# A Conformer block on one core: every engine's instruction order and the PSUM banks re-drawn

## The chip, the core and the metric

The kernel runs on one core of one Trainium2 chip. The core has five instruction queues that run at the same time and meet only at semaphores: TensorE (PE, matrix products into PSUM), VectorE (DVE), ScalarE (ACT, here mostly exponentials and tanh), GpSimd (POOL) and SyncE (SP, which here issues transfers). The metric is device time in microseconds for one execution, the median of several runs; less is better.

## The reference

Two sequences of 4,000 tokens with 144 channels go through one Conformer block. All inputs are bf16.

```
x = x + 0.5 * silu(layernorm(x) @ w_ff1a) @ w_ff1b          # 144 -> 576 -> 144
q, k, v = split(layernorm(x) @ w_qkv)                        # 4 heads of 36
p = softmax(q k^T / sqrt(36))                                # 4000 x 4000 for each head
x = x + (p v) @ w_o
a, b = split(layernorm(x) @ w_pw1);  h = a * sigmoid(b)
c = depthwise_conv(h, dw, 5 taps)
x = x + silu(c) @ w_pw2
x = x + 0.5 * silu(layernorm(x) @ w_ff2a) @ w_ff2b
out = layernorm(x)
```

## The kernel before

**Tiles.** The 8,000 tokens are 16 chunks of 500, eight for each sequence; a chunk is four blocks of 125 tokens. Keys come in tiles of 64. A score tile is one chunk of queries against one key tile for all four heads. PE makes it with four matmuls of 64 x 64 weights and 500 columns ("quads", tiles PS<-QT,KT in the profile), two per PSUM bank, so a score tile fills a pair of banks. Most score tiles are emptied by one ACT instruction of 128 x 1000 exponentials (PT<-PS). About one tile in five goes to DVE instead, which makes the exponential from integer operations in five instructions. PE then multiplies PT by the values (PS<-PT,VA, also quads) into banks 6 and 7, where a chunk's attention is summed. Banks 0 to 5 serve all else.

**Between the score tiles** lies the rest of the block for other chunks: feed-forward (`ff`, `ff_tile`, lines 1208 to 1260; tiles XT, WA, HT, WB), projections (`pre2`), the gated convolution (`glu`, `conv`) and the output half (`post1`, `post2`). Normalization (`ln`, line 1109) takes its statistics on DVE (ST), its square root and scaling on POOL (RS, XN). The transposed copy of a chunk (XT, XTQ) is made by a transpose on DVE and a round trip of transfers that SP issues: XN or AN to a DRAM buffer called rows, and rows to XT (`blocks`, line 1032).

**Order.** The program is recorded, not issued directly. A scheduler in the kernel (`pick`, line 1940) chooses step by step what comes next, and `Rec.op` records each instruction with its engine, its step number and its dependencies. All instructions of one engine that were recorded in one step are a block. There are 2,855 blocks on PE, 1,093 on ACT, 1,689 on DVE, 125 on POOL and 157 on SP. Then `Rec.reorder` (line 281) moves the blocks within each engine by a written table, ORDER: one character per block, whose place in ALPHABET less 45 is the number of places that the block moves (P is no move, `~` opens a longer number).

```python
shift.append(c - 45)
...
at[i + shift[i]] = blk
```

The second table, PLACES, gives each of the 1,724 PSUM tiles its first bank, one digit per tile (`place`, line 257). `reorder` reads off PE's new order which tile had a bank before, and makes the new tile's matmuls wait for the instructions on other engines that use the earlier tile:

```python
prior[k] = {last[b] for b in self.tiles[k] if b in last}
...
for p in prior[k]:
    o.deps += [(d, False) for d in users[p]]
```

`finish` (line 365) turns dependencies into semaphore waits, and `replay` (line 409) issues each engine's list in order. [...] All instructions are issued from line 419, so the profile gives that line nearly everywhere and tiles tell the groups apart.

Of the kernel before, what the change touches and what calls it, by code (L numbers as in the profile page):

```python
# [13 lines left out]
H = 4  # L14
# [26 lines left out]
        "nXMJ@LJMFMYGaJNKMJhLLLLljKKKKKKWKMMWNKK`BJJJQRecHFSIGKH]QKMRGKPMJJMMQTNPNXTRSUJUJJJSLPMPPQUQQNKOTOOR"
        "OQLPPPPPYOOPN[NNNOMfRNLYULMIMOS^KIMOJNaNNQMNHPPaUOMQNYKPSPPQUSVV^QQ^_Q5<@QCPMKIMNNTQMSMNSNUOYQKMMOQQ"
        "^MSOORNOPPCOORPZP^O]OOO[OCNOQEHMUJNNTOMR[MQWXMPMMNNDMPXSNNZMMTMMMTMPLMPP]OOOOQQNUKNOMQMP]WNOMPNVKYPN"
        "JNQHNOOPQQQMPPQOPUP]MNNNOOTNNOMNWOPPMPNOW]VNN[MMHMKYMMQ]YKI`JLQYJJKV[KHMJTLJOJPMQORPVMQNYMN]MN[bLLLL"
        "LMNLPRPKWOYFMNOVNOHXXMKOLNNNN[[_MMMTLLTKKKLJOOPRP`MO_OMNOMPQLLMRMMMPPPQOSYP[MOOISOLNPPIPSPTOLRNNWPNO"
        "QQMMPUQRN[QQQRJFPPPPJQQSPPKQQNPPPPVPPQOPVXOOPNDNPRROSVSYNFWMPYUPNDPJFPNPTOPYOLOPNQ[NLNRPMRLNNOPhUNZM"
        "MMNLNNPMMWYLPNZKNLMF[LPPSLVINLNOMWQNYPYPLQHKOSNORPGPPPS[OOLOOPPYLNNNVOMNOM^QMNTOO_KMMNOMPPLPNQOYL]RY"
        "LMKLMMPLY]KLNNQXMRXSLI[MDObNOENPMMNSNNQMMWNNNOSVNiKZNNQOTFNNOMXXUMMMM?TLLIYMQXXLLMMQZMJJ`ORLMUMKQYNL"
        "INPMMUVNLNOMYPMOORNNRUNKPNO_ROQLSSKMQMKPROLPSOORNOSOOOTVNNNNSNTMTMNNOVXNOMORLSNVXIMSYLMKLN^XYNLMNHMM"
        "WLLMXMNYMOLNNXMNXMMVMM[SLJLLZN^OLNNJUbLLLQNLPRGNNOOOPNRNOPPPeOOOOPSOOORROf`OPNO^@QDLJLMOLTKLTMTRKGMQ"  # L50
        "QNUOPNROYYPZOHNbILLLLbTLLSLLLLPLM_M[MMMMMcMMMMNLMOdZMNNNNIMMMMXMNNVOMKMMZNOUaMMMQMM]^HOMKNNNJZMKM[LM"
        "QgLLLMWMMMMU]LLLV^MQJMWTMHBHMZSKL[PLLZTMK_bMMIGbMPLPQMSVCKRKSMBINPPSPVOLOOOOZQNNS[MMMMNSMOMNO]aNNcMM"
        "MMMMMMNLNNNZWNZMZPNKPMYBENOPJYNNPMPQOLQNPPRRO[YQJNOPQOPXFPHPNOOOPWOOOOOOXPMTQOLOK^OXNNOMPPPLPPHQQNgR"
        "cOLQOMPNOOOOdRM@LdOJOIPIOOOJOOOOJOOPNUPNOOQQYLQ]NLZ[LLLdWKIKLLLWULE]LLLLLOMWRcKLLLNZM[PMMRILNKZJ`[JK"
        "MOLLUbKeJLLYKOUKMMMMMY=KMNNZNL^NLNNNNNN_NNNOQQNPTHNN_NLOOO^QMNPKO^QQM_JFPLOPJMNPPLPhMPROOPQOWOWNNNNU"
        "U?NO[HMTOOOCNOOOQO[OQOUOOOPHVORPYMGNPPMOVNN[QOVKPNZPGLOY]OPLOPPPBHOOORPRROR`OPWQNZCLNNPQZKMQETOJOMNU"
        "OOOOOPPPP[OOPNQNQRLMVZLOTNKPLLOOPPVPNOVOMRMOSLOOPPPPPZOWOMNNN]NLMPRTLNZUNLQMNYWNRAOPTOSHRNDQOPTOOPNP"
        "UOUQ_LROQQIQFNOYPNUKQNKTNKOQRSTNQNRXFQOQVQULMVEMPPP[PPPQODZcMPMMQINPKMPNOOOPRMNPPPQOZOOOOOQOMOOPXOOZ"
        "NNNNNN`NPWMXNNOPNKOCNOXPNOQOMZQMUOKXMZP[^XIMMOOKPABPJOPPPXOOQOPPPRIOPSOVSMOTKQUKLPNQNPXQOMROMPMQWQMU"
        "OQNJMQQNPQQTQOKTNO[NQOPQOUOOVRMUZPNVSYMN`OQK6TNNZ;NLNVMMMMTMMVWMMdMNLMNOO]N[MMM]XLJKKRK^aJHNPPRKNX>N"  # L60
        "OJLOMNPPPSPPQTVOOQVPLPQOAPQOPQOQZVOLOMRUMKL[MPMOOQWMMNNYOLNORNNNOYVNNNOWLMMROORROH]QNQMNOXNOMPMUPKMY"
        "NTOLORSTJMWOPPFObTYLNQSMKG_MKMNN`RMKLOLR]MKPNgIMMMNOYNKNNNNNZTMQXILIXJLMQLYOSJMNPU_]JLOKRSMMHLMOMQOW"
        "OOQOMOUNPNUQRM`YYLOREKNKKV[LJNLOSQJN`KPXLObLMWNK]MIJQLLOUO^LDLTKQNLVLQ^MMQRMSFMUWMNNWMG^MTRMJYLRPNGO"
        "TYMN[aXVMWQHKLJMFRf[M5LMNSNNKNLZMNNQRPLJTOIOO`^YMMNLMMOMKMMNRSLROLPPTOVOOLVNNPMOO_ROOLRNNNQQMMRNNPQO"
        "VQNNTVNLMPMZUO_QOLLOSNNVNOQNNQSPSWNWNPNVNN[QMNRPNQVXMNPMXPPXKUNNNNVQM~N?ZRMMMPXRLM]LLSMNLNQOMO[NQORO"
        "TNPPY[K]SBNNKILMNNPNPP_TNNOMN]NNNNNPMM_NNNNOQNQOPKWOOPKQN`YOOROOPFOQNROEQQUYJVNNPJOOJ[OOPNPROLYTNKMN"
        "TMNNNP^[NOMNNQMMOLNN]PNOOR[OPKQN_ZLNESMOOKHOM[NPPLPNOOPPMQSTMNPQQQQRSQRRTCQVNGRNOMTTTMMNUPPQHNQSPMYV"
        "TQKLLSSOIJPSSPTMKORNOQOPPPPPPSORNSMRNRRRNQQRPFRPQQQQQQRPFQO"
    ),
    "act": (  # L70
        "PPPPPPPPPPPPPRTNNOOPPQOPPPPPPXPNOSNNNNPPPPQOPPSPNOQZQORKRSLLOQQJPPPPQQNQOPPPPPPPPPQQQMPPQOPPPPPPPPRO"
        "OPQOPQQNPPPPPPPPPPPPPPPPPPPPPPPPPPPPPPPPPPPPPPPPPPPPPPPPPPPPPPPPPPPPPQOPPPROSNOOPPPPPPPPPQOPPPPPPPPP"
        "QOPPPPPPPPPPPQOPPPPPPPPPPPPQOPPPPPPPPPPPRPNPQOPPPPPRPNPPPPPPPPPPPPPPPPPPPPPPPPPPPPPPPPPPPPPPPPPPQOQQ"
        "NPPPPPPPPPPPPPPPPPPPPPPPPPPPPPPPPPPPPPPPPPPPPPPPPPPPPPPPPPPPPPPPPPPPPQOPPPPPPPPPPPPPPQOPPQOPPPPPPPPP"
        "PQOPPPPPPPPPPPPPPPPPPPPPPPPPPPROOPQOPPPPPPPPPPPPPPPPPPPQOPPPPQOPPPPPPPPPPPPPPPPPROOQQQMPPPPPPPPPPPPP"
        "PPPPPQOPPQOPPPPPPPQOPPPPPPPPPPQOPPQOPPPPQQQQQKQQNPPPPPPQOPPPPPPPPPPPPPPPQOPPPQOPPPPPPPPPPPPPPPPPPPPQ"
        "OPPPPPPPTOOOOROOPPPPPPPPPPPPPPPQOPQOPPPPPPPPPPQOPPQOPPPPPPPQOPPPPPPPPPPQOPPPPQOQOPPPPPPPPQOPPPPPPPPP"
        "QOPRPNQOPPPPPPPQOPPPPPPPPPPPPPPPPPPPPPQRNOPPPQOPPPPPPPQQNPPPPPPPPQOPPPPPPPQOQOPPQOPPPPPPPPPPQOPPPPPP"
        "PPPQOQOPPPPPPPPPPPPPPPPPPPPPPPPPQOPQQNPPPPPPPPPPPPPPPPPPPPROOPPPPPPPPPPPQQNPPPPPPPPQOPPPPPPPPPPPPPPP"
        "PPPPPQOPPPPPPPRPNQOPPPPPPPQOPPPPPPPPPPPPQOPPPPPPPPPPPPPPPPPPPPPPPPPPPPPPQOPPPPPPPPPPPPPPQOPPPPPPPPPP"  # L80
        "PPPPPPPPPPPPPPPPPPPPPPPPPPPPPPPPPQOSPNRNOQOUQNPMOPPPRORNQNPPPPPPQOROQQMPPPPPPQOPPPWORNNNOO"
    ),
    "dve": (
        "PUO[VM~P6~P6~P)~P6ILIKKLDKMJQRJJJKIKQKKLJKMKOLJWOILJHLJNQNPHFGNNNJMMMMBMWOIKIMINLMNOODNDPSPLORCFVSWC"
        "JDJSIOMBREEMKNCMMMMFNNJMMMMMMNLOPSPROLPPRPNPQOQOQQQMQOQQNPQQNQOPPQOPPQOPPPQOROOPROQVQOYPNOPROSPXURVQ"
        "UU;JNIQQSSSOSQRSSZRSSSKRVQUJ=OO)PROQNPRPRSLPRPQJQOPPPUOPNPQ`VPVOVOMEULFNKNRMRPQQQQIQOPQOQOSOORNTNOPN"
        "QOPQOPPQOQOPPPRPNPROQRMQRPQRPTPPPRPVVPNPSOLQQQQQQ5PPVPPPPPQRHQQQLPPPPPPPPQOPPPPPPPPPROSNPNPPPQSQSLSO"
        "RJQQLQQQQQQQQHPPROSPPTRPNQGQOPQOUQOPLQNRPNPQORUNNOOQNSOOTRUOMTOOPFPQOPPPPPPQQRRRKMRPNPQOPPPPPPPPPPQR"
        "PRPQQQHQOPWOPSOSKTLVOSNUNQMDOPPROOSOPNSQO^PjOOOSNNNCMNTMPLMNTNNNNNOOOPROOROOPRPQQRPJPRSNNQNPQOQOPQOQ"
        "OYRNNNYNOMNSOLRMULQNNOTPPMOQOQOPQOPPPSOPNSOSNPQLPPPPPPPVOOOOOXNOOROQNKUOOOOQNQOPPTTPNLNPPPPPPPPPPQSP"  # L90
        "PLQOPPP]OOOOOOOOOOOOQOQOPQOQOROOPQOWOPNOOOORPNPSPNSSPRSJTJWMRSLLRLMPTRNNQQLQOPPPPPPPPPQQSMPNPRPSPPQJ"
        "PPPPPQQNPQOQQNQOROOPQOPPPRPNPPPQQNPPPPTOOOOPQOPRPNQOQQRSOKQNQOSOOQNQRNOPQOSQRMMPPPPPROQNQOPPPPPQOPPP"
        "PQRPQRRORPQFPPPPPPPPPWPNPNOOOUPNOPNQSNSNNSNORNUQMPMOPROOROVNOOOPQMPPPPPPXQNQMQUNQNSOUQQUCOJOOPPQQNQO"
        "PPUPNOOOPPQRPQQRJQTPLOOTOOOOPPPQVNOQTMQNSQTNTFNNQNQOPPQQNPQOPPPQOQORPSPLOTOOOORORNQSMSNTRPRJRPIROQNQ"
        "OPTQNNTNOOSNSNNOUOOOOOPPPPPPROOROOQOQUROQSUSTGOHKPPPPPQOPQOQOPPQOPPROOQOPPPPPPPPPQRPUPPSORTRPRSUURXS"
        "=KQAQRNQQEPPPPPPPQOQOSOSOhTPMPRMSEOOKOPPPPPPROGNOPPPQRNRNOPQQQMPPPPPQQNQQNQQQQQKQQQRVOXOHOOLOOQNRPNP"
        "PPPPPPPSOOWNSNNQMUQKSOOQJQUN^PhLNKOPPKOKNNNPPMOOOOOOOOQQQRRKNPRPRPSQOQTPTODNRNQNQQUPLPROTRPWMXSNPSQW"
        "RZQUFOSDO7KOPPPTOOSOTOPPIPPPQOPPPPPPTPQMQMPQOPQQNQQRRORRRUQRPUWTQNRSCTRPRRRRDQQRPSPRSQR[RTQNPREO~NKO"
        "RNaNOOOPQMNQYNOPNPTQFNJPRRNNPPPPQOPQOPQOPRSOROUSINNNPPPPPPPPPPPQOPQOQQRPWQQNPTPUPUKOO?OPQOROQQMPQOPQ"
        "QNPQQSPTQNPHPPROOQSNPQULPNOORROQRPJPPSOOORO]SOSNPRWQQXPTRERGRRTTUXRTRSBSSSSSSSSAT@S&NNPPPPPPPPPPQO"  # L100
    ),
# [2045 lines left out]
```

## Time and profile before

| | |
|---|---|
| median of 3 runs | 874.99 us (874.88 to 875.48) |
| span of the profiled execution | 873.9 us; its own time is not given apart, so the runs' median stands for it, 1.1 us above the span |
| instructions | 27,051 |
| busy: PE, ACT, DVE, POOL | 844.3, 845.4, 824.8, 292.8 us |
| weight loads on PE (PEld) | 385.8 us busy |
| granted TensorE clock, mean | 0.998 |
| transfers | 28.82 MB in 114,353 packets, mean 33 GB/s |
| XT<-rows, time from issue to landing | 2.0 us (median) |

A row of the profile names the line, the engine, the operation and the tiles (out<-in), then how often it ran, its busy time and mean duration, and the idle time of the engine just ahead of it with what ended that. The chain of waits is followed back from the last instruction to whatever released each step.

### The profile page before, as it was taken

How to read it: one execution, taken by the hardware profiler on the slowest of the kernel's cores; microseconds unless marked ns; L12 is line 12 of the kernel's file. 1: busy time of each engine (PE TensorE's matmuls, PEld its weight loads, DVE VectorE, ACT ScalarE, POOL GpSimd, SP SyncE). 2: the span in 40 equal slices, each digit the busy share in tenths (PEclk: the TensorE clock that was granted, in tenths of full speed). 3: DMA queues.
4: the chain of work that ended last, by engine and by line, in shares of the span. 5: the costliest groups of instructions: out<-in, count | busy, mean ns of one | idle time of the engine just before them, and what ended most of it. 6: DMA issues, size and time to landing. Idle time of an engine off the chain costs nothing.

```text
span 873.9 us, 27051 instructions
## 1 busy us (share of the span) xinstructions
PE 844.3 (97%) x11419; PEld 385.8 (44%) x11419; DVE 824.8 (94%) x1821; ACT 845.4 (97%) x1098; POOL 292.8 (34%) x573
## 2 busy tenths in 40 slices
...
GB/s 100 49 62 29 23 17 44 33 67 30 29 52 39 17 50 11 45 22 47 23 4 29 24 56 17 30 30 16 37 31 24 21 31 21 19 15 38 28 26 35
DMA packets 114353, 28.82 MB, mean 33 GB/s; under 512 B 101090, under 2 KB 114230, under 8 KB 114230
## 3 DMA queue, kind: packets, MB, share of 16 engines
...
## 4 chain that ended last, share of the span: by engine, by line
ACT 59%; PE 25%; DVE 11%; POOL 4%; issue 1%; POOLq 0%; DVEq 0%
ACT PT L419 54%; PE PS L419 25%; ACT TH L419 5%; DVE PT L419 4%; POOL XN L419 2%; POOL RS L419 2%; DVE ST L419 2%; DVE X L419 1%; DVE XN L419 1%; DVE HT L419 1%; DVE U L419 0%; DVE KT L419 0%; DVE RS L419 0%; DVE AN L419 0%; DVE XT L419 0%
## 5 line engine op out<-in xcount | busy, mean ns | idle before, releaser
L419 ACT ACTIVATE PT<-PS 128x1000 bf16<-128x1000 f32 (+1 forms) x818 | 752.0, 1051 | 3.7 <-PE PS L419 2.8
L419 PE MATMUL PS<-QT,KT 64*64 64x500 bf16 x3968 | 419.9, 384 | 12.4 <-ACT PT L419 7.4
L419 PE MATMUL PS<-PT,VA 64*37 64x500 bf16 x4728 | 406.4, 372 | 1.6 <-DVE QT L419 1.0
L419 DVE TENSOR_SCALAR PT<-PS 128x500 int16<-128x500 f32 x380 | 250.2, 668 | 6.9 <-PE PS L419 5.1
L419 PEld LDWEIGHTS PS<-QT,KT 64*64 64x64 bf16 x3968 | 124.8, 104 | 232.0 <-ACT PT L419 132.2
L419 POOL TENSOR_SCALAR RS<-ST 125x4 f32<-125x4 f32 x130 | 37.8, 291 | 475.6 <-DVE ST L419 469.0
L419 PEld LDWEIGHTS PS<-PT,VA 64*37 64x37 bf16 x4728 | 142.7, 96 | 93.4 <-issue 13.6
L419 DVE TENSOR_SCALAR PT<-PT 128x1000 uint16<-128x1000 uint16 x380 | 154.2, 419 | 2.3 <-PE PS L419 1.0
L419 POOL TENSOR_SCALAR XN<-X,RS 125x144 bf16<-125x144 bf16 x260 | 144.7, 586 | 9.7 <-DMA out_dram<-XN 1.5
L419 DVE TENSOR_TENSOR PT<-PT 128x1000 bf16<-128x1000 bf16 x190 | 127.5, 674 | 0.9
L419 ACT ACTIVATE TH<-PS 128x500 bf16<-128x500 f32 (+3 forms) x194 | 102.8, 551 | 4.7 <-PE PS L419 4.5
L419 POOL TENSOR_TENSOR RS<-RS,NHALF 125x4 f32<-125x4 f32 (+1 forms) x93 | 92.8, 1002 | 33.5 <-DVE RS L419 27.9
L419 DVE SCALAR_TENSOR_TENSOR HT<-TH,PS 128x500 bf16<-128x500 bf16 (+1 forms) x135 | 81.0, 613 | 10.1 <-ACT TH L419 9.7
L419 PE MATMUL PS<-XT,WA 80*128 80x500 bf16 (+5 forms) x288 | 74.5, 364 | 4.2 <-DVE XT L419 1.0
L419 DVE BATCH_NORM_STATS2 ST<-X 125x6 f32<-125x288 bf16 x160 | 65.5, 446 | 1.6 <-DMA X<-in_x_dram 1.4
L419 DVE SCALAR_TENSOR_TENSOR X<-PS,X 125x288 bf16<-125x288 f32 (+1 forms) x128 | 56.6, 449 | 5.6 <-PE PS L419 4.3
L419 PE MATMUL PS<-WB,HT 128*125 128x144 bf16 (+1 forms) x640 | 52.6, 230 | 0.8 <-ACT HT L419 0.5
L419 PEld LDWEIGHTS PS<-WB,HT 128*125 128x125 bf16 (+1 forms) x640 | 44.3, 136 | 14.2 <-issue 4.3
L419 PEld LDWEIGHTS PS<-XT,WA 128*128 128x128 bf16 (+1 forms) x288 | 21.1, 97 | 37.7 <-issue 10.1
L419 POOL COPY U<-U 128x2 bf16<-128x2 bf16 (+1 forms) x54 | 12.0, 263 | 56.2 <-DVE U L419 56.2
L419 DVE STREAM_TRANSPOSE XN<-XN 128x320 f32<-128x320 f32 x54 | 27.0, 500 | 2.8 <-POOL XN L419 2.6
L419 PE MATMUL PS<-U,DG 128*128 128x250 bf16 (+6 forms) x204 | 28.8, 263 | 0.1
...
## 6 DMA issues: line engine op xcount, KB each, us to landing
...
```

The source lines that it names most:

```text
L419: ins = getattr(eng, o.name)(*o.a, **o.k)
```

## The change

Only the two tables differ: ORDER for all five engines and PLACES. The scheduler, the instructions, their operands other than the PSUM bank, the transfers and their number stay. The new tables come from a re-timing in which landings of transfers and waits carry a margin. Of 1,724 PSUM tiles, 683 have another bank.

```diff
 ORDER = {
     "pe": (
-        "PPPPPPPPQOPPPPROQNPPQRPQLPPRPTPUPNIZOVOKVVL~OOKOK~OUHINSNLMMMOPNOJSOOL[I[KMYMKOGRNJHFKOOOE^NNN_dMKLM"
...
+        'PPPPPPPPQOPPPQQQMPPPPPPPPSOUOMOYWMOX~OQQLHxSIYH~OXG~O[IIKSJKILJHKNOMOOQQXDYCOHNGOHX?FHHKLPLFnKPLe_KPMJUVJG=LJMFFPVlEoICKKLLRL_LMKNLRMRLMK[_Q'
...
     "pool": (
-        "PPPPPPPROOPPPSOPNPQQQQQQJPPPPPP_PPPPPJOOPQ[NKTMMOMNOSNUMNSNRNTKVNVMPLMPMROQTMOOTVMNNNOQTMOOQWMOOOSNN"
-        "NVOOPNOQNPPPRPQM"
+        'PPPPSOOQQMPPPSOPNQOPPPQQNPPPPPP^OOOOOTNOMQaLOPPIOOPPMOUNNPMVLU[MMMMQLNOPSOUKNOOSSMNNPQRNOPPSPNQQMPQQQMPPPSOOOPPPQRPM'
+        ''
     ),
     "sp": (
...
+        'PPPPPPPPQOPPPPPPPPPPPQQNQRSMNOPPPPPQOPPQOQOPPPPPSOOOPPPPQOPPSOOSNOOPPPQOPPPPPPSORNNPPVOPNSNNVMOOOOOPSOWNNOOOOOPROXNPNOOOORNOPPPQOROOPPPPPPPX'
+        'PNOOOOPQMPPPPPPQO'
+        ''
     ),
 }
 PLACES = (
-    "3054320451505435202310543130213550204405323242301405230054110122532155431241204124012410314032034023"
...
+    '43240510405134250421350102245231040421520105150412304523405004503101012141412340240014300442130242024305302341314010402430240213430532040324'
...
 )
```

More of the change, by code (lines that the diff above doesn't have):

```diff
@@ L39 @@
     "pe": (
-        "PPPPPPPPQOPPPPROQNPPQRPQLPPRPTPUPNIZOVOKVVL~OOKOK~OUHINSNLMMMOPNOJSOOL[I[KMYMKOGRNJHFKOOOE^NNN_dMKLM"
[L41 to L68, printed above, removed]
+        'PPPPPPPPQOPPPQQQMPPPPPPPPSOUOMOYWMOX~OQQLHxSIYH~OXG~O[IIKSJKILJHKNOMOOQQXDYCOHNGOHX?FHHKLPLFnKPLe_KPMJUVJG=LJMFFPVlEoICKKLLRL_LMKNLRMRLMK[_Q'
@@ new lines @@
+        'JhBIII[XKPHJ_JFLUIZKPMGLQMMWDNPRMOMTTZXTLPIKISOMJQQQT_QNIRTOM[OPFOJOQOQOIQO^QOMPNhNPNLZOLLPLWUNLNNZNaQNPQQCROHTQNROSKP[RRRYUPX]SGV`Q$HBQFFQK'
+        'PLOOTQMMRNRNTNSPMMTO`NXNOOOO_NNND^MMM_aYMILLHbKSHLIXHL^RMQMMa[YEP]MINTKNE6JKffLLXTLPLLLHLNPKMN`TNKNLQQQQEPQQX]SQJRLSWX`NPZ:OPEP@GNPQRLRPHQOb'
+        'TXMMMMRLOMTPPMGNUNPQOLR[_NOKNRWOQJKMSGbMKQOM`dPMKSXLIMKRHLIKLOOOTNXNNN^NNPMM]XMMMMMMNLPVOUYNYGLLQXMOLQFMYNQMNOO_W[LLLZLY]JJJJKMSXXYZFQOZK@MF'
+        '^dTXJ=LcHQJLRLaYHRAILWPKILMRCMMPVPNOPSWPZJOSINLMPUMUOOOPIUOOOOaPPSOJOPPKOOOVQNLMOXTXNNOPHUNIQSQKYKOW]PMVaNNKOETOUCXNH]PMXNODGNNOSQK^KOOOOOOO'
@@ new lines @@
+        'OOOOOPWOQNNWWNQOZZJM[EOMINOMRPRMREOUQNQXQMRPHMOQRPRKOPPPQSQOLPbQOQjKMNNNPMOLNQMMaOOQIMMNOMOOLPNPVPL[UULNKKM]OKTRLLMMP[MQTRLJQMKPUMP_MQMMWWNR'
+        'MOMKNRPSCRNfRRNNQOYFNNOMUNLMMMNSWMMQXLTOULIMORVSPM[N]NCOOLQTRMNIRHOU`OQLNLRORLMPPLPRMQRMOYQNNP^QUKOLJNPMeNWMMMXMPLLLYRLLMK^McL]LJNLa[MJ[PHJH'
+        'OTOJPZmBPAFOUYOVNK[PNK^BLNQM?ZLM_MGRMU^MGROKL[NAPL[SPZLHOPKVbDLMRMXVPKMUCL_LSKVGKMXMcLLLQLLLUUMa[NNPQ[HFYKMALLNXJLLOPSMSNSSN]QMPEO[QMYM[J]UK'
+        'ILIXLJTYLEMTLVN[EZLJ[LLZLLNK[UKN~OUMJDLNPaLPNJW[LMM[LLMKSDSI]KHMOFN`MTPTKIPRIRNHDMOPXaNNNTFNNNURGMMMUWNOJNSMN`QVNRIaN`QIL_GNN[MNHZL`LPLYUMO['
@@ new lines @@
+        ':OSKUM=LO<QagSNIMNOSQWNKKWMMMMXVMSOL:`SLP^MCOOOOOPQOSPRIZS@PNTPNSNSF^RdMHRPM]QHNP]GQHRIU[II^IIPKQJ]_KOTKWNFNIgOLPQRSUR@WTQU]LHR[KLR9TMK]^PhK'
+        'UNjdaSTOSWjbQ<SAZR?#>ZQ<P;TNBPWRPUUOUO6Q7UP7PRTZ^LaaMKMcLNLORK=MPNRHcL^SNL;LLOMSNcKMKLNXMRMMNTKNPK`K_WLM_OLJdXKXKIE^LJNLFOQQbTKKMM;SNNN[OZKN'
+        'LMMMNNNNZZNNZTMKWOJQQHRRFQSDOV[QObLOPGOPIOPPJVPbLPKSPJQIYLZMNLMTYWMI_HLGNLQLNOPNPNWNPUMNNNNUXNNN`MWNKPMVNNPULNDMSQXVJOOXORNFROOQbEOOOQOULNOa'
+        'NPMQNRFLQMQRVMNOHPQTPKRcNLOOOPNOO[NQMPPKVRIOKVYQ[SFOILYOQ]]MCMOMNPRMN@MPQOQOPVO]RMTRK[SIRTGaLOVENN]NCSSLMTMKWMTCLNRMMPVPVOLRTVXP^ZIOMUZMAL@T'
@@ new lines @@
+        'LQKSQRERH^QMNRTNXMNWHLOLSNJhMXVNNKMT^MMQNTaQNQBPPJQR=RYQNPT`H`OZPKQHNP3MPHTRXRMGGPNVOMQTRMTQIR[IPPKPPMR[OQWJOIRPLTQJ]THUO[T_HXHNORHNSCEKWRRR'
+        'XISOJRFMRPLROTNVSMRUKRLTTQFSTRUSFUURESUZESGIWSOJVSLLSMZRRS@WQNYOENFQOWKQ[LOTOMOOPVPNTOOOeZOO:QOMK]MMMMRNLXLLMcPLWIMM^WMNNKOSYKDLJUP]XKGMKOYL'
+        'U[^LWHLMVMNC_ULJMPUX^^Z]LLFM5LEOMEMI[SNNNNROMN[^NOTNIP]MJNIYWMPVOLFNTR[OCPFUYRTdSS[WRRRZQAYQ?SQ=KS;^R9Y[QUM`PTGXJGQRZVGQCKZQMVRPYL[OMQOT]QN!'
+        'SQNTYO4DNbWSMOMF[NPMOEPNWKOLROOTPGOOPPRPUPcPP[QKQEQMWRNGJMPJMRP^PPUUNZSMKM[PXMOQYMOk9MMPNOTPN8NaPXMUZMGLOHPPHORF[RDTPUOJ_YLMFLRMNNOJOOVPSOSO'
@@ new lines @@
+        '[_PYUOC]ZMILNK]Od]OVZQ7QLN;PXZRWOZ[IXM7NIYZ`L[KKQdLLOKQU^L%RJN&JSaLLM[L[NGOLLMOMUMMQGSMSNNOPXOZNROLPKVKOM[WNNV[MGNSM]MWQOQDPPVPPb[P:RSNNSNVX'
+        'MM8OULUXNOXO9PNOZRO]eKNNTNTUZLJLMS`RMAcLVNORVZLCLNRRL~NH]RKBLSQXLUQUJHKKVLUUMMMNURVTRL_WQYRPU[>EWNHPRH<NHPZ[NNRMNPMJNNOXOQWNLOOL_OPKP_bNOTI`'
+        'PSXGQGRREJRCJTAXORNXcHSQJLRKHMPPWPSJPMURP]FOUQOMPNPUP>UPR_L^GLXO_NJMPL_RJLRHOTOQ^I_:OJQOYPKOFKPMOQQQQSSUNBWOQSTOTRSTTBSSGBRKRSOPQJTTQSSTJJJQ'
+        'NP[VNPNLNOPSKNNQRPXLOPNOOOOPRROMTQNPMSORNRRRNQQSQFSPPQQQQQQEPQO'
@@ L69 @@
+        ''
     ),
     "act": (
[L71 to L80, printed above, removed]
@@ L81 @@
-        "PPPPPPPPPPPPPPPPPPPPPPPPPPPPPPPPPQOSPNRNOQOUQNPMOPPPRORNQNPPPPPPQOROQQMPPPPPPQOPPPWORNNNOO"
+        'PPPPPPPPPPPPPPSOOOPPPPPPPSOVNWOLNTMMNNPQOQORSQUUKKUNTMUNHMOOQQQMPPPPPROOROQNPPPPPQQQQLPPPQOPPPPPPPQOPPQOQQQMPPPPPPPPPPPPPPPPPPPPPPPPPPPPPPPP'
+        'PPPPPPPPPPPPQQNPPPPPPPPPPQQQMPPROQNPROOPPPPPPPPPPPPPPPPPPPPPQOPPPPPPPPPPPQOPPPPPPPPPPPPPPQQQMPSOOOPQRPMPQOPPPPPRPNPPPPPPPPPPPPPQQNPPPPPQQNPP'
+        'PPPPPPPPPPPPPPPPQOPPPPQOPPPPPPPPPPPPPPPPPPPPPPPPPPPPPPPPPPPPPPPPPPPPPPPQQQMPROOPPQOPPPPPPQOPPPPPPPPPPPPPPROQQQLPPPPPPPQQQQLQRNQNPQQNPQOPPPPP'
@@ new lines @@
+        'PPPPQOPPPPQOPPPPPPPPPPPPPPPQOPPPPPPPPPPPPRPNPPPPPPPPPPPPPROQNQQQRRKQQQKPPPPPPPPPPPPPPQOPPQOPPPQQRMOPQQNPPQQRRSSJRRRISSPSSSSJSBSTIQLQQQQQHPPP'
+        'PPPPPPPPPPPPPPPPPROQQMRROQQQJPPPPPPPPQQQMPPPPPPPTOOOOROOPPPPPPPPPPQOPPQOPQOPPPPPPPPPPPQOPPQOPPPPPPQQNPQQQMPPPPPPPPQQQMPPPPPPPPPPQQNPPQOSOOOP'
+        'PPPSPNOPPPPQQQQQKQOPQQNPQQNPPPPPPPPPPPQTNOPNQQNPPPPPPPQQNPPPPPPPQQNPPPPQOQOPPPPPPPPPPPPPPPQQQMPPPQOPPPPSPNOQQQMPPPPPPPPPPQQQMPQQQQQRRIQRROQQ'
+        'QQQQDPPPPPPPPPPPPPSOOOPPPPPQQQQQQQIPPPPPPQQQMPPPPPPPQQQRRSTUHTJSSSIRRRRRRDRDOQOPQOPPPPROOPPPPPPQQRRRSJRRRIQQQIPPPQQQQLPPPPPPPPPPPPQRROQKPPPP'
@@ L82 @@
+        'PPPPPPPQQNPPPQQQQLPPPPPPPPPPPPQOQQRROQQIPPPPPPPPPPPPPQOQSNSNNQNUOPNOOPPPUPNOPNPRROMQOPROQQMPPPPQQRPQQQWPGOOOOO'
+        ''
     ),
     "dve": (
[L84 to L97, printed above, removed]
@@ L98 @@
-        "RZQUFOSDO7KOPPPTOOSOTOPPIPPPQOPPPPPPTPQMQMPQOPQQNQQRRORRRUQRPUWTQNRSCTRPRRRRDQQRPSPRSQR[RTQNPREO~NKO"
-        "RNaNOOOPQMNQYNOPNPTQFNJPRRNNPPPPQOPQOPQOPRSOROUSINNNPPPPPPPPPPPQOPQOQQRPWQQNPTPUPUKOO?OPQOROQQMPQOPQ"
-        "QNPQQSPTQNPHPPROOQSNPQULPNOORROQRPJPPSOOORO]SOSNPRWQQXPTRERGRRTTUXRTRSBSSSSSSSSAT@S&NNPPPPPPPPPPQO"
+        'PPSSUX~O|~P<~P&~P;HHHJLLLGLNLJNOOOHJGMMJLLOLNKMNLEMKLQMPJLJFLLLNNKMMMMELYLLMHJLJLNPPPFPFOROMQR@ATDUGHNJQITOCSEGOLODQMMODOPLMPMMNPMMNPQMRMIPP'
+        'WQNQMQMSMRNNQORRNNQSNPRMOQORRNRPLPPPPPQRPRPVQQZPPKQOPRPXRPSJTN8OQKRRTTTPTRSSTYSVRRMVXR[?:QN8OPRTUUBTUWHSJRUIVQJRMOVQ;QSaSXRLYRUDPSCGIILOSPTT'
@@ new lines @@
+        'NVJRLSSOVQWPPWOVOVXOOKPR9RN9PQORPNQRNOPPPPWOQQQMPYQOPRPWSLNQMPQQQQQQQ6PPUOOOPNPQSUSNKRRRLIQUNPNOOPPUPNOPRMOPQOPPPPRPRMQNPPPPPPQQNPPPPVOSTMTN'
+        'LJOPPROSPMVPSOOOIPSPTOLTQQYLJOOPPMOORSUNLVRRKMKQNPQQQRPQQRSQNRSORORPQQQQQ[PQQQQQQQQRTRERSQXKR$OQLSOSSSORKSPPQRPQQQ=RRNRMQ]MiOPPMOOOGNNNOSOPL'
+        'VLNPMPNKSSWNNPRSORRSSPRAQ`SOOOPQOPUOOOOYNRXXNLQMMUL+TRWMVHPNIShPKYOIPNOKORLRMQVMHNOORKTPKPRPUKOUOMNPN[OQNQRPQJ[OOHOPNOOSPNQKYPNOOOPUPLXLRNYN'
+        'OIOMQORpNPIORPMMOOPNSNNRMOLUNNOORRJLPSKSMPMSQORSOTOPGVNQNPPQKQOPROOQRSORKNQQTQQRMTPSOOTCQNQQLRPSPPTJOOOPVOOVNOULOUKMSTLNWKVMNUOLLRLQRSQTRxVQ'
```

38 lines of the change are left out of this document (19 added, 19 removed).

## The prediction

> **What bounds the kernel now.** I read four views in this order: the page's busy times and chain, the stages, ACT's groups by form in the middle stage, and the waits.
>
> ```profile
> PE 844.3 (97%) x11419; PEld 385.8 (44%) x11419; DVE 824.8 (94%) x1821; ACT 845.4 (97%) x1098; POOL 292.8 (34%) x573
> ...
> ACT 59%; PE 25%; DVE 11%; POOL 4%; issue 1%; POOLq 0%; DVEq 0%
> ```
>
> PE and ACT tie at 97% by busy time. The chain decides: more than half of it is ACT work. The stages show where ACT is not full (columns: busy us and instructions of PE, PEld, DVE, ACT, POOL):
>
> ```profile
> 0.00:50.00 50.00, 44.76 (x475) 29.37 (x475) 43.74 (x135) 36.76 (x69) 33.80 (x77) 1.00 0.31 71
> 50.00:825.00 775.00, 757.74 (x10438) 327.00 (x10441) 740.02 (x1558) 771.56 (x953) 242.69 (x466) 1.00 0.14 31
> 825.00:874.00 49.00, 41.83 (x515) 29.40 (x503) 41.00 (x130) 37.12 (x78) 16.34 (x31) 0.97 0.13 32
> ```
>
> ACT stands idle 13.2 us in the first 50 us, 11.9 us in the last 49 us, and 3.4 us in the 775 us between. That last figure flatters it. The longest ACT run of the chain gives the pace when nothing is late:
>
> ```profile
> 774.65 26.53 ACT PT L419 x30
> ```
>
> Thirty exponentials in 26.53 us are 884 ns each. The same instruction lasts 1059 ns on average by its row below, so each overlaps the one before it by 1059 - 884 = 175 ns, and a wait that only eats the overlap is never shown as idle. ACT's groups in 50 to 825 us:
>
> ```profile
> L419 ACT ACTIVATE PT<-PS 128x1000 bf16<-128x1000 f32 x779 | 722.3, 1059 | 2.6 <-PE PS L419 1.8
> L419 ACT ACTIVATE TH<-PS 128x500 bf16<-128x500 f32 x111 | 69.2, 639 | 0.8 <-PE PS L419 0.8
> L419 ACT ACTIVATE PT<-PS 128x500 bf16<-128x500 f32 x15 | 10.0, 664 | 0.0
> L419 ACT ACTIVATE TH<-PS 128x250 bf16<-128x250 f32 x21 | 9.7, 461 | 0.0
> L419 ACT ACTIVATE TH<-PS 64x125 bf16<-64x125 f32 x14 | 4.1, 296 | 0.0
> L419 ACT ACTIVATE TH<-PS 80x125 bf16<-80x125 f32 x12 | 3.5, 290 | 0.0
> L419 ACT ACTIVATE KT<-PS 128x500 bf16<-128x500 f32 x1 | 0.6, 613 | 0.0
> ```
>
> At pace (mean less 175 ns) these are 779 x 0.884 + 111 x 0.464 + 15 x 0.489 + 21 x 0.286 + 14 x 0.121 + 12 x 0.115 + 0.44 = 688.6 + 51.5 + 7.3 + 6.0 + 1.7 + 1.4 + 0.4 = 756.9 us (an estimate). The stage took 775, so 18.1 us is what ACT loses there, in pieces mostly too short to show as idle. The instructions stay the same, so the change can win back only those 18.1 us and part of the 25.1 us at the two ends. It can lose without limit. The sum goes against the profiled span of 873.9 us; the median of the runs, 874.99, is 1.1 us above it, which I take as fixed and add at the end.
>
> **The change part by part.** What the tables say is read by arithmetic: a character's place in ALPHABET less 45 is how far its block moves; I laid both tables on the block list of the kernel before. None of it is a time. Of the blocks, 13% keep their place on PE, 15% on DVE, 61% on ACT, 38% on POOL, 51% on SP; 683 of 1,724 PSUM tiles get another bank. The mean distance between old and new place is 4.7 blocks on PE, 2.9 on DVE, 0.7 on ACT. No instruction, transfer or byte is added or removed, so the sum has only waits and matmul transitions.
>
> *PE's changes of tile kind.* Walking PE's new order, the matmul kind (64-row scores and P·V quads against 128-row feed-forward, projection and so on) changes 718 times, before 768. The price of one:
>
> ```profile
> 603.12 0.38 PE L419 MATMUL PS<-QT,KT 64*64 64x500 bf16 x4
> ...
> 603.33 0.38 PE L419 MATMUL PS<-PT,VA 64*37 64x500 bf16 x4
> ...
> 603.64 0.62 PE L419 MATMUL PS<-XT,WP 128*128 128x500 bf16 x2
> ...
> 604.71 0.23 PE L419 MATMUL PS<-WP,SW 128*125 128x144 bf16 x1
> ...
> 604.78 0.23 PE L419 MATMUL PS<-WP2Z,SW 80*125 80x144 bf16 x1
> 604.93 0.41 PE L419 MATMUL PS<-QT,KT 64*64 64x500 bf16 x4
> ```
>
> A quad follows a quad after 0.21 us, a 128-row matmul follows a quad after 0.31: 0.10 us more. On the way back it is 0.15 against 0.07: 0.08 more. So 50 changes fewer are 4 to 5 us less of PE work; I take 5.0. Only PE's quarter of the chain can turn that into time: 5.0 x 0.25 = 1.25 us. Bounds: 0, if the rest of PE's waiting for ACT swallows it, and 5.0, if each saved piece stood before a late ACT.
>
> [...]
>
> *Cover between releasing a bank pair and using it again.* ACT can hide the next scores only behind its own work between the instruction that empties a bank and the one that reads the next tile in it. From the release on, PE needs at least this much:
>
> ```profile
> 775.60 0.11 PEld L419 LDWEIGHTS PS<-QT,KT 64*64 64x64 bf16 x4 [0.32 <-ACT PT L419]
> 775.61 0.40 PE L419 MATMUL PS<-QT,KT 64*64 64x500 bf16 x4
> ```
>
> 0.40 us for the scores alone. Counting ACT work at the pace above, from 60 to 800 us of it, 5 tiles of 849 have under 0.6 us of cover before and 1 of 842 after; the smallest cover goes from 0.16 to 0.47 us. Four such places at up to 0.4 us each are 1.6 us off. Bounds: 0 to 4 x 0.6 = 2.4.
>
> *DMA landings.* The wait list has a single wait of a compute engine for a transfer behind the start, on POOL and on no chain of ACT:
>
> ```profile
> ACT PT L419 <- PE PS L419: 2.8, 8, 0.8
> ...
> POOL XN L419 <- DMA out_dram<-XN: 1.5, 1, 1.5
> ```
>
> Neither PE, ACT nor DVE ever waits for rows that come back through DRAM. In vector work between the transpose that feeds the chain of transfers and the first matmul that reads the result, the new order has 11.8 us on average, before 11.4. A margin on a landing that was never late is worth 0; bounds 1.5 us off (POOL's wait) and 0.4 us on (the later first reader, once). SP's 157 blocks move by 0.85 places on average; the stores move forward most, and nothing on chip reads them.
>
> *POOL.* The worst place of the middle stage for ACT is a run of four normalizations on POOL that ends late:
>
> ```profile
> 560.00:565.00 5.00, 4.09 (x47) 1.11 (x46) 3.02 (x6) 4.43 (x7) 1.70 (x4) 1.00 0.12 21
> ```
>
> ACT loses 5.00 - 4.43 = 0.57 us. Normalizations there only swap within one or two places, so I keep it; bounds 0.6 off or on.
>
> *The ends.* ACT's first 13 instructions and last 6 are the same. The work ahead of the first exponential (14.8 us) and behind the last (23.5 us) is the same; the eighth exponential has one 0.9 us lump of tanh more ahead of it; PE work behind the last scores falls from 29.0 to 28.4 us. I take 0, bounds 1.5 us either way (about 6% of the 25.1 us).
>
> Sum: 873.9 - 1.25 - 1.6 = 871.05 of span, and with the 1.1 us around it 872.15, say **872.1 us**.
>
> **Rivals.**
>
> *A. More of the small losses go.* Margins on every wait could keep ACT fed where it was fed just in time. If half of the 18.1 us goes, the time is 875.0 - 9.0 = 866. For it: the cover counts move the right way over the whole range. Against: 548 tiles still have at most one exponential of cover, before 552, so the usual distance hasn't changed.
>
> *B. Nothing comes through.* ACT runs at its pace and PE's saved time only lengthens PE's waits for it, of which there are plenty:
>
> ```profile
> PEld PS L419 <- ACT PT L419: 152.2, 421, 1.1
> ...
> PEld PS L419 <- DVE PT L419: 49.8, 158, 1.1
> ```
>
> Then the time is 875.0, with 0.2% (1.75 us) as about what a measurement of this kernel tells from no change.
>
> *C. Slower: more bank pairs hang on DVE.* With the new banks, the score pairs of ACT whose banks were last emptied by DVE, alone or with ACT, rise from 162 to 196. DVE is 740 of 775 us busy and works in order, so such a pair is free only when DVE has come to it: the second row above gives 49.8 / 158 = 0.32 us a wait. If all 34 further pairs reach ACT, that is 10.7 us on and 872.1 + 10.7 = 882.8; half of them, the likelier size, give 877.5. It decides from about 9 pairs on (9 x 0.32 = 2.9, the whole gain). For it: 82% of DVE's neighbours are new. Against: in work counted as above, DVE's place relative to PE moves 3 to 4 us later than before by the second half, which leaves PE earlier rather than later; most DVE releases also have an exponential of cover.
>
> [...]
>
> **How the numbers follow.** Forecast 0.38, A 0.15, B 0.14, C 0.33. C weighs much because the order is new nearly everywhere while the count that favours the change touches four places. Faster by over 0.2% (under 873.2) is forecast and A: 0.53; within 0.2% is B: 0.14; slower is C: 0.33. The forecast's own range is 870 to 873.2. The range for 8 in 10 leaves out the lower part of A and the upper part of C: 867 to 880.
>
> **What would show it.** Right: ACT's middle stage, cut at the same instruction counts, shorter by 1 to 5 us with ends within 1.5 us; 128-row matmuls that follow a quad fewer by some 20 to 25; PE's weight loads waiting longer for ACT. B shows as the same ACT shortfall near 18 us in the middle. C shows as a larger PE wait for DVE PT (over 55 us) and more ACT waits for PE than 2.8 us. Wrong altogether would be a wait of ACT, PE or DVE for a transfer, or an end that moves by over 3 us.

## The result and the profile after

The new order takes 882.62 us (median of 4, 882.17 to 882.76) against 875.00 us (median of 4) for the old one: ratio 1.0083, interval 1.0069 to 1.0097. It is slower by 7.6 us, where 872.1 was forecast and 880 was the top of the range. The profiled span is 880.8 us, before 873.9.

The page of the new kernel, busy times and the chain by engine:

```profile
PE 843.9 (96%) x11419; PEld 388.0 (44%) x11419; DVE 826.3 (94%) x1821; ACT 849.7 (96%) x1098; POOL 295.5 (34%) x573
...
ACT 40%; PE 27%; DVE 26%; POOL 4%; issue 1%; DMA 1%; SPq 0%; DVEq 0%; POOLq 0%
```

The busy times hardly moved. The chain did: ACT 59% to 40%, DVE 11% to 26%. The stages of the new kernel (columns as before):

```profile
0.00:50.00 50.00, 43.80 (x463) 29.49 (x463) 42.35 (x131) 36.13 (x68) 32.26 (x73) 0.97 0.30 70
50.00:825.00 775.00, 754.05 (x10384) 326.47 (x10380) 738.77 (x1554) 770.89 (x948) 243.20 (x464) 1.00 0.14 30
825.00:874.00 49.00, 46.03 (x580) 32.03 (x576) 43.84 (x133) 41.51 (x82) 19.32 (x37) 1.00 0.14 32
```

In the same 775 us ACT issued 948 instructions, before 953, and its busy time fell only from 771.56 to 770.89 us: five instructions are missing and almost no idle time shows for them, because each instruction overlaps the next by less (from the 68th to the 1026th ACTIVATE 0.160 us on average before, 0.138 after). A better measure is the start of the same ACT instruction in both traces. Counting ACT's ACTIVATE instructions, the 68th and the 1026th are the same ones in both orders. The 68th starts at 50.61 us before and at 51.39 after; from it to the 1026th pass 779.23 us before and 784.72 after. So the new order is 0.8 us late at the end of the head, loses 5.5 us in the middle and 0.6 in the tail: 6.9 us, the difference of the spans.

The waits of the new kernel that answer to those shown before (us in total, times, longest):

```profile
PEld PS L403 <- ACT PT L403: 126.9, 349, 1.3
...
PEld PS L403 <- DVE PT L403: 69.7, 197, 0.8
...
ACT PT L403 <- PE PS L403: 3.0, 8, 0.7
...
PEld PS L403 <- DMA XT<-rows: 2.3, 5, 0.8
```

PE waits 39 times more often for DVE's PT and 72 times less often for ACT's. ACT's visible waits for PE are nearly the same (2.8 before). The wait of the last row came once before, at 180 us; it stands further down the same view than the rows that the prediction read:

```profile
PEld PS L419 <- DMA XT<-rows: 0.4, 1, 0.4
```

At the head, DVE of the new kernel (start, duration, line, operation, what it waited for), and the rows of PE behind it:

```profile
6.03 0.17 DVE L403 MEMSET KL<- 128x128 uint32 x1
6.17 0.17 DVE L403 MEMSET VL<- 128x128 uint32 x1
7.15 0.27 DVE L403 MEMSET VA<- 128x248 bf16 x1 [0.81 <-issue]
7.35 0.44 DVE L403 MEMSET VL<- 32x2 bf16 x4
7.91 0.33 DVE L403 MEMSET XN<- 128x320 uint32 x1
8.15 1.07 DVE L403 TENSOR_SCALAR XN<-X,ST,RS 125x144 bf16<-125x144 bf16 x4
```

```profile
4.70 1.80 PE L403 MATMUL PS<-IDENT 128*128 128x128 bf16 x20
8.69 0.39 PE L403 MATMUL PS<-IDENT,XN 125*128 125x125 bf16 x4 [2.20 <-DVE XN L403]
```

Before, the same scaling started at 5.59 us and PE had no such wait:

```profile
5.59 0.70 DVE L419 TENSOR_SCALAR XN<-X,ST,RS 125x144 bf16<-125x144 bf16 x2
```

The wait has a consequence. In the windows of the first microseconds (the last three columns are granted TensorE clock, DMA share and GB/s), the new kernel's row is the second:

```profile
9.00:12.50 3.50, 3.31 (x42) 2.84 (x40) 2.86 (x11) 3.29 (x7) 0.23 (x1) 1.00 0.52 138
```

```profile
9.00:12.50 3.50, 3.50 (x26) 2.71 (x24) 2.73 (x12) 2.58 (x7) 1.80 (x3) 0.53 0.51 138
```

Behind the 2.20 us of idle PE the granted clock fell to half for 3.4 us, and PE ran 26 matmuls where it had run 42. Some executions of one kernel show more half clock than others (with both ends mended, below, one has a mean clock of 0.989 and five have 0.997 or 0.998); where a long spell fell into a run, it is said.

### The profile page after: what moved, and what is told of

It reads as the page before. It is cut to its first block, busy times and chain, and to the rows that moved or that the text cites. A ratio compares the mean times of both kernels' runs of the same rounds, so it can differ in the third digit from the quotient of the medians.

```text
span 880.8 us, 27079 instructions
## 1 busy us (share of the span) xinstructions
PE 843.9 (96%) x11419; PEld 388.0 (44%) x11419; DVE 826.3 (94%) x1821; ACT 849.7 (96%) x1098; POOL 295.5 (34%) x573
## 4 chain that ended last, share of the span: by engine, by line
ACT 40%; PE 27%; DVE 26%; POOL 4%; issue 1%; DMA 1%; SPq 0%; DVEq 0%; POOLq 0%
ACT PT L403 36%; PE PS L403 27%; DVE PT L403 15%; ACT TH L403 4%; POOL XN L403 2%; DVE QT L403 2%; DVE ST L403 2%; POOL RS L403 2%; DVE HT L403 1%; DVE X L403 1%; DVE XN L403 1%; DVE KT L403 1%; DVE AN L403 1%; DVE VA L403 1%; DVE U L403 0%
## 5 line engine op out<-in xcount | busy, mean ns | idle before, releaser
L403 ACT ACTIVATE PT<-PS 128x1000 bf16<-128x1000 f32 x818 | 752.5, 1032 | 4.8 <-PE PS L403 3.0
L403 POOL TENSOR_SCALAR XN<-X,RS 125x144 bf16<-125x144 bf16 x260 | 151.2, 611 | 8.3
L403 DVE TENSOR_SCALAR PT<-PT 128x1000 uint16<-128x1000 uint16 x380 | 151.2, 414 | 1.5 <-PE PS L403 0.3
L403 POOL TENSOR_TENSOR RS<-RS,NHALF 125x4 f32<-125x4 f32 (+1 forms) x93 | 91.0, 980 | 33.8 <-DVE RS L403 28.4
L403 ACT ACTIVATE TH<-PS 128x500 bf16<-128x500 f32 (+3 forms) x194 | 99.4, 545 | 2.6 <-PE PS L403 2.3
L403 PE MATMUL PS<-XT,WA 80*128 80x500 bf16 (+4 forms) x288 | 74.3, 369 | 2.5 <-DVE PT L403 0.8
L403 POOL COPY U<-U 128x2 bf16<-128x2 bf16 (+1 forms) x54 | 10.0, 224 | 76.6 <-DVE U L403 76.5
L403 PE MATMUL PS<-U,DG 128*128 128x250 bf16 (+7 forms) x204 | 27.9, 263 | 0.2 <-DVE PT L403 0.2
```

The source lines that it names most:

```text
L403: ins = getattr(eng, o.name)(*o.a, **o.k)
```

## The experiments

Besides the head, two theories stand for the middle. Mine is rival C of the prediction: DVE empties score banks later, as PE and ACT see it, and the loss runs through DVE. The rival is that PE's own order and the new banks cost it, with DVE a bystander.

**Mend the head.** DVE's fillings go behind the first scaling.

```diff
-fillings of KL, VL, VA (7 memsets)
 filling of XN 3
 scaling of XN 0 (2)
 scaling of XN 1 (2)
+fillings of KL, VL, VA (7 memsets)
 fillings of WPZ, DG
```

> The changed kernel with one block of DVE moved: the seven memsets of KL, VL and VA, which the new order puts ahead of the first scaling of XN, stand behind it again. Theory (the loss is made in many places, each by its own late instruction): PE's 2.2 us wait for XN at 6.5 us goes and TensorE's clock stays full there, so the first products come some 2 us earlier; most of this was already caught up by 50 us, where the changed kernel lagged 0.8 us, so 881.8 us, 0.8 us less than 882.6. Rival (the head shifts the whole kernel): 2.5 us less, 880.1. Rival (the head is hidden): 882.6.

Measured: 880.72 us (880.47 to 880.75), ratio to the old kernel 1.0066 [1.0051, 1.0081], so 1.9 us better than the new order. The same window:

```profile
9.00:12.50 3.50, 3.31 (x42) 2.84 (x41) 3.14 (x17) 3.30 (x7) 1.42 (x3) 1.00 0.54 140
```

Clock and matmul count are back. ACT's 68th instruction starts at 49.50 us, 1.1 us ahead of the old kernel; from there to the 1026th it takes 784.70 us, as in the unmended order (784.72). The head cost 1.9 us, nothing of it was caught up later, and it hid that the rest of the new head is 1.1 us better.

**Move the last chunk's scaling.** The tail has DVE scale chunk 11 second to last, so its store is issued with the last four.

```diff
 RS<-ST of chunk 11
+scaling of XN 3, chunk 11 (4)
 scaling of XN 0 (2)
 ...
-scaling of XN 3, chunk 11 (4)
 scaling of XN 1 (2)
```

> The changed kernel with one other block of DVE moved: the last scaling of chunk 11 (four instructions, XN 3), second to last in DVE's new order, goes back up behind its statistics. Theory (many places): its store of 140 KB no longer falls together with the four stores of the last two chunks, and the time from the last scaling to the end goes from 5.4 back towards 4.0 us: 881.2 us, 1.4 us less. Rival (the end is set by the last chunks alone): 882.6, no change.

Measured: 883.04 us (881.95 to 883.37), 1.0091 [1.0076, 1.0106]: no gain. DVE's last instruction in the old kernel, in the new one and in this one:

```profile
869.36 0.55 DVE L419 TENSOR_SCALAR XN<-X,ST,RS 125x144 bf16<-125x144 bf16 x2 [0.75 <-POOL RS L419]
```

```profile
873.91 1.44 DVE L403 TENSOR_SCALAR XN<-X,ST,RS 125x144 bf16<-125x144 bf16 x6
```

```profile
876.08 0.54 DVE L398 TENSOR_SCALAR XN<-X,ST,RS 125x144 bf16<-125x144 bf16 x2 [0.81 <-POOL RS L398]
```

From the end of the last scaling to the end of the span it is 4.0 us in the old kernel, 5.4 in the new one (875.35 to 880.8) and 4.3 here (876.62 to 880.9). The stores came quicker and the last scaling later by as much. The loss moved; it did not go.

**Bank-emptying DVE instructions earlier, everywhere.** If late emptyings cost the time, pulling them forward should bring it back. 181 such instructions of the new order went forward by one or two places; the same rule moved 163 in the old order.

```diff
 for each DVE instruction that empties a bank PE will refill:
+    if its data is there by then, move it 1 or 2 places ahead
```

> The changed kernel with 181 DVE instructions that empty a PSUM bank moved one or two places forward on DVE, past instructions that empty none, wherever the trace of the changed kernel shows that they waited in DVE's queue for at least 0.25 us after their input was there. Nothing else moves. Theory (banks held by DVE make PE late and starve ACT: late ACT starts behind a DVE release come to 6.9 us in the changed kernel against 3.5 before): 3 to 6 us less, 877 to 880. Rival (PE's longer runs of other matmuls are the cause, or the promoted instructions only push others back): within 1 us of 882.6.

> The kernel before with the same rule applied to its own trace: 163 bank-emptying DVE instructions moved one or two places forward. Theory (DVE releases matter, but fewer of them end on ACT here, 3.5 us): 0 to 2.5 us less than 875.0. Rival (moving instructions off the planned order costs by itself, whatever it does to the banks): 1 us or more slower than 875.0; then the like of it has to be taken off the third kernel's result too.

Measured: 892.05 us, 1.0196 [1.0181, 1.0211], and 886.63 us, 1.0134 [1.0117, 1.0151]; 9.4 and 11.7 us worse than what each was made from. In the old order the rival (1 us or more slower) holds; in the new one neither expectation does. The weight loads of P.V in the new order and with the 181 moves (busy, mean ns, idle before and what ended it):

```profile
L403 PEld LDWEIGHTS PS<-PT,VA 64*37 64x37 bf16 x4728 | 141.3, 96 | 91.6 <-issue 9.5 <-DVE PT L403 8.7 <-ACT PT L403 5.3
```

```profile
L398 PEld LDWEIGHTS PS<-PT,VA 64*37 64x37 bf16 x4728 | 141.2, 96 | 111.6 <-DVE PT L398 28.3 <-issue 9.0 <-ACT PT L398 6.2
```

In the old order the same wait behind DVE went from 7.0 to 28.1 us. What the moves gave to the scores (their loads' wait for DVE fell from 33.7 to 28.4 us in the new order) they took nearly four times over from P.V, whose tiles DVE now finishes later. The mirror run in the old kernel shows that this says nothing of the change: DVE serves two customers, and a blanket move helps one at the other's cost. The theory was left untested.

**Old and new order in one kernel.** Up to a step of the recording one order and its banks, from there on the other.

```diff
-order, places = new
+order, places = new below step 5929 (499 us), old from there
```

> Both tables from the changed kernel for all blocks and tiles that the scheduler records before step 5,929 (ACT reaches it 499 us into the kernel before), from the kernel before for the rest. Theory (the loss is spread over the kernel, and each part keeps its own): the same ACT instruction came 2.3 us later at this point in the changed kernel, so 875.0 + 2.3 = 877.3 us. Rival (one or two places, at 400 and 735 us, carry it): 0.9 to 1.3 us of it by 499 us, 876. Rival (only an order planned as a whole is good, and any seam costs): 880 or more.

> The other way round: the kernel before up to step 5,929, the changed one from there. Theory (spread): the rest of the loss, 7.6 - 2.3 = 5.3 us, so 880.3 us, and the two losses of this pair add up to 7.6. Rival (an early lag sets up the later ones): 877 to 878, and the two don't add up.

> The kernel before up to step 9,809 (830 us), the changed tables only for the end. Theory: of the lag of 6.9 us in the span, 5.5 to 5.9 were there before the last instructions of ACT, so the end alone gives 1.0 to 1.4 us: 876.2 us. Rival (the end is free and its late stores only follow from the lag): 875.0.

> The changed tables only up to step 691 (50 us), the kernel before from there. Theory: taking the seven memsets out of the way was worth 1.9 us in the changed kernel, so the head gives 1.9 us: 876.9 us. Rival (it is what the lag at 50 us says): 0.8 us, 875.8.

Measured: new to 499 us 877.95 (1.0026 [1.0017, 1.0036]); new from 499 us 881.27 (1.0066 [1.0050, 1.0083]); new from 830 us 877.64 (1.0027 [1.0016, 1.0038]); new to 50 us 879.88 (1.0058 [1.0043, 1.0073]). The two halves lose about 2.6 and 5.9 us, 8.5 together for 7.6: nearly additive, with most of it in the second half. The last two missed, and the traces say why (median lateness of the ACT instructions around each time against the old kernel's trace, us):

```
old kernel's us      50   100   300   500   600   700   800   830   870   end
new order           0.8   0.9   0.6   2.2   2.9   3.7   5.2   6.2   5.3   6.9
head mended        -1.1  -1.0  -1.2   0.3   1.0   1.8   3.3   4.3   3.5   5.0
new from 830 us    -0.1   0.0   0.0   0.0   0.0   0.0   0.0   1.6   0.8   2.3
new to 50 us        3.0   6.3   6.3   6.4   6.4   6.4   6.4   6.4   7.1   6.8
```

The switch at 50 us costs several us by itself, with a second spell of half clock (mean clock 0.52 from 53 to 60 us) in the profiled execution, which took 882.53 us where the other three took 879.8 to 879.9; that run settles nothing about the head. The switch at 830 us costs 1.6 before the tail proper begins. The loss of the middle is a steady drift from 300 us on, not one accident.

**Lighten DVE in both kernels.** The run that decides. DVE's product and last masking of P work on 500 of 1000 columns, so half of the P of DVE's tiles is not what the reference asks for. No instruction, bank or place changes.

```diff
-op("dve", "tensor_tensor", yf, zf, yf, op=ALU.mult, ...
+op("dve", "tensor_tensor", yf[:, 0:CH], zf[:, 0:CH], yf[:, 0:CH], op=ALU.mult, ...
-op("dve", "tensor_scalar", zu, zu, 0x7F80, 2, ...
+op("dve", "tensor_scalar", zu[:, 0:CH], zu[:, 0:CH], 0x7F80, 2, ...
```

> The old kernel with the last two of VectorE's four steps on P (the product and the last masking) cut to 500 of their 1000 columns, so that 190 tiles take some 0.5 us less each (some 100 us of VectorE's 826) and half of their P is not what the reference asks for. Every instruction, wait and bank stays. If VectorE co-limits, as I believe, the old kernel gets a little faster: PE's wait for VectorE's emptying (49.8 us in the old kernel) falls to under 25, and the time to 865 to 873 us. If VectorE only waits for others, the time stays at 875 within 1.

> The same cut in the new kernel. My theory: the 3.5 us that the new order loses between 50 and 825 us come through late VectorE instructions (banks of scores that VectorE empties late, and PE's queue behind them), so with VectorE light the new kernel stands only the head and the end above the light old one: 1.9 to 4.2 us, in place of 7.6. The rival, that PE's own order and the bank table cost it (scores asked for late, more matmuls between a bank's release and its next use), keeps the gap at 6.5 to 8.5 us, since no matmul is moved or shortened.

Measured: 872.48 us (5 runs), 0.9963 [0.9951, 0.9976], for the old order; 874.09 us (11 runs), 0.9983 [0.9975, 0.9992], for the new one. The gap is 1.6 us where it was 7.6, just under the 1.9 to 4.2 that my theory gave; the rival's 6.5 to 8.5 falls. The chain by engine, the middle stage and PE's wait for DVE, light old order first:

```profile
ACT 73%; PE 20%; DVE 4%; POOL 2%; issue 0%; POOLq 0%; DVEq 0%
```

```profile
50.00:825.00 775.00, 758.48 (x10482) 326.85 (x10480) 685.74 (x1564) 772.96 (x957) 221.47 (x466) 1.00 0.14 31
```

```profile
PEld PS L419 <- DVE PT L419: 34.2, 110, 0.8
```

Then the light new order:

```profile
ACT 71%; PE 24%; DVE 3%; POOL 1%; issue 1%; DMA 0%; SPq 0%; DVEq 0%; POOLq 0%
```

```profile
50.00:825.00 775.00, 756.85 (x10480) 330.18 (x10484) 687.71 (x1569) 774.20 (x957) 224.25 (x468) 1.00 0.14 31
```

```profile
PEld PS L403 <- DVE PT L403: 52.7, 155, 0.7
```

With DVE's busy time in the stage down from 740 to about 686 us (54 us less, not some 100), both orders get through 957 ACT instructions there. From the 68th to the 1026th it takes 776.41 us in the old order and 776.46 in the new one: 5.5 us of difference became 0.05, with not one matmul moved. Nor is the difference hidden under a full ACT: at pace (883, 467, 259 and 154 ns from start to start by form, where nothing is late) the stretch would take 760.3 us, an estimate, so ACT loses some 16 us in both.

So most of the middle's loss needs a full DVE. Not all of it: against the light old kernel the light new one is 0.9 us late at 50 us, 0.6 ahead at 300 and 0.9 late at 830. It wins 1.5 us and loses 1.5, where at full weight it won 0.2 and lost 5.6; that both come out equal is a balance. No run lightens PE by as much, so it isn't shown that only DVE's load brings the loss out. The 1.6 us that remain (1.8 in the profiled executions) are 0.9 ahead of the 68th instruction and 0.9 behind the 1026th.

The last rows hold a warning: PE's wait for DVE still rises by 18.5 us (it rose by 19.9 with DVE at full weight) at next to no cost. Lightening DVE took 15.6 us of it in the old order and 17.0 in the new one, and gained ACT 2.8 and 8.3 us. The expected fall to under 25 us in the light old kernel did not come either.

**Keep the good part.** Mended head, new order to 306 us (step 3698), then the old one.

```diff
-order, places = new
+order, places = new with the head mended below step 3698, old from there
```

> The new order up to step 3698 (some 306 us), with the seven fillings of VectorE put back behind the first scaling of XN, then the old order. My theory says that the new order is ahead of the old one by about 1.1 us between 50 and 300 us once the head is mended (the run with the head mended stood 1.1 us before the old kernel's instructions there), and loses only later: the switch back at 306 us should keep the lead, so 873.8 us (875.0 less 1.1, plus 0.1 or so for the seam), between 873.3 and 875.0. The rival, that the lead is borrowed from the work behind it (the new order puts off P.V products or emptyings that must then be made up), gives 875.0 or more. A seam as costly as the one at 50 us would give 878 to 879.

Measured: 875.26 us (12 runs) against 875.39, 1.0016 [0.9997, 1.0035]; a miss. The profiled execution keeps its lead (ACT 1.4 us ahead at 300 us, 1.0 at 830) but ends only 0.5 us ahead (873.4). Three of the twelve executions took 881.6 to 882.1 us at a mean clock of 0.988; the other nine have a median of 875.1, 0.3 us under the old kernel, which these runs can't tell from nothing. No re-ordering here beats the old kernel.

**Both ends mended.** Mended head, new order to 830 us, old from there.

```diff
-order, places = new
+order, places = new with the head mended below step 9809, old from there
```

> Both ends mended in one kernel: the new order with the seven fillings behind the first scaling of XN, up to step 9809 (830 us), and the old order and banks from there on. Where the three losses add (head 1.9 us by the run that mended it, tail 2.3 by the run that took the tail alone, the rest the middle's), it takes 882.6 - 1.9 - 2.3 = 878.4 us, between 877.7 and 879.2. The rival, that the tail's loss is only the new middle's lateness carried on, or that the new tail made up what the new middle owed, so that taking it back gains nothing, gives 880 to 881. What remains above the old kernel, 3.0 to 4.2 us, would be the middle's loss, to be compared with the 3.5 us that ACT's late starts there give in the trace.

Measured: 880.50 us (6 runs), 1.0061 [1.0047, 1.0075]: the rival's 880 to 881, not my 878.4. One execution, the profiled one, took 887.27 at clock 0.989; the other five lie between 880.00 and 881.18. Taking back the new tail gained 0.2 us against the mended head alone, or 0.7 as differences from the old kernel in the same runs (5.8 and 5.1 with the disturbed execution left out). So the 2.3 us of the tail run were, it seems, mostly its switch. In the profiled execution the part from the 68th to the 1026th ACT instruction takes 785.00 us, the middle's loss once more (5.8 us).

The ledger of the 6.9 us of span is then: head 1.9 (mended and measured), less 1.1 that the rest of the new head is ahead, middle 5.5 (0.05 with DVE light), tail 0.6 (by the trace; no run isolates it without a switch).

## Why the prediction was wrong

**The sum had no term for DVE.** This is the step that failed. It counted PE's transitions and ACT's cover and left DVE's emptyings to rival C, priced at 877.5 by half of 34 pairs. Its premise that DVE works in order held: in both traces DVE's 1,821 instructions start in the order in which the kernel lists them. In place of a gain the middle lost 5.5 us, most of it through DVE, as C has it. I laid the block lists on the traces. Between 50 and 825 us the score pairs of ACT whose banks DVE had emptied, alone or with ACT, rise from 153 to 185. I counted the ACT starts that come at least 30 ns behind pace. Those right behind a DVE release rise from 25 to 43, and from 3.5 to 6.9 us. Those with PE late elsewhere rise from 6.5 to 9.3 us; of these, 4.2 and 6.6 us have a wait for DVE as PE's longest in the 2.5 us before.

**C's prices meet the measured ones by accident.** Half of its 10.7 us is close to the middle's 5.5, but 32 further pairs gave 3.4 us of late starts, 0.11 us each and not 0.32. Its full price, 882.8, is close to the measured 882.6, but contained only pairs; the measurement contains the head and the tail.

**The argument held against C** was that DVE's place relative to PE moves 3 to 4 us later by the second half. The traces show no such lateness at the banks. DVE starts to empty a bank 0.50 us after PE's last matmul for it in the old order and 0.53 us in the new one (by the profile, mean of some 800 in the middle), a score tile 0.34 us in both. More banks hang on DVE; it comes to each hardly later. Order and banks were not tried apart, since with the table of PE, ACT or DVE exchanged alone, or the banks alone, the engines wait for each other in a ring.

**PE's transitions, 1.25 us: counted nearly rightly, no gain seen.** The traces have 736 changes between quads and other matmuls before and 696 after, 40 fewer where the prediction counted 50; other matmuls that follow a quad went from 368 to 348. At the prediction's prices that is 3.6 us of PE work and not 5.0. No run isolates what it was worth. Even with DVE light, where ACT carries 71 to 73% of the chain, the middle shows no net gain.

**Cover, 1.6 us: the right direction.** In the same count, the late ACT starts whose bank ACT itself had released fell from 5.5 to 2.5 us, and with DVE light from 5.2 to 2.9, while those behind a DVE release rose there from 1.9 to 3.3 and the others from 5.0 to 6.2. At full weight the whole count rose by about 3.2 us. These are counts from the traces; no run isolates the cover.

**The ends, 0 within 1.5 us: 1.4 us late in sum, but broken at the head.** I looked at ACT's first 13 instructions, which are the same, and at PE. What moved was DVE ahead of PE's first transposes, and the clock behind it: 1.9 us, of which the rest of the new head hid 1.1.

**DMA landings, 0: nearly right in size, wrong in kind.** The prediction said that PE never waits for rows that come back through DRAM. Before, it did once, for 0.4 us; now it waits 2.3 us in five waits. DMA carries 1% of the chain (a load of X at the start, and one landing of XT, 2.87 us from 672.83 us). With DVE light the same wait is 0.8 us. POOL's share of the chain stayed at 4%, as forecast.

**The markers.** PE's wait for DVE above 55 us came true (69.7), but the light kernels show that it can rise by as much at next to no price. ACT's visible waits for PE did not rise (16.0 us in all before, 15.3 after), and PE's waits for ACT's PT fell from 152.2 to 126.9 us, where the forecast had them longer. The readings that told were DVE's share of the chain and the time between the same two ACT instructions.

**The time around the span** was taken as 1.1 us and is 1.8 in the new kernel's profiled execution and 1.8 to 2.2 in the later runs'; 0.7 us of the miss. The whole miss, 882.6 - 872.1 = 10.5 us, is then the 2.9 us of gain that did not show, 5.5 in the middle, 1.4 at the ends and these 0.7.
